# Second unit's scores ahead of the first weights, weight shifts ahead of the maximum, fewer MLP products in the step where the MLP begins

## The chip, the core and the metric

The kernel runs on one core of a Trainium2 chip. Its engines run side by side, each through its own list of instructions in order: TensorE (PE, matrix products; its weight loads are listed as PEld), VectorE (DVE), ScalarE (ACT), GpSimd (POOL) and SyncE (SP, which here only starts transfers). They wait for each other by semaphores. The metric is the device time of one execution in microseconds; the kernel before takes 1659.19 us (median of 3 runs, 1656.96 to 1659.2).

## The reference

Attention that keeps the 32 largest scores of each row, and an MLP behind it, all in float32. The input has 8 batches, 8 heads, 576 rows and a head size of 64; the MLP is 512 wide with a hidden layer of 2048.

```python
scores = scale * np.matmul(q, k.transpose(0, 1, 3, 2))
kth = np.partition(scores, -top_k, axis=-1)[..., -top_k:-top_k + 1]
scores = np.where(scores >= kth, scores, -1000000000.0)
scores = scores - np.max(scores, axis=-1, keepdims=True)
attn = np.exp(scores)
attn = attn / (np.sum(attn, axis=-1, keepdims=True) + 1e-09)
out = np.matmul(attn, v)
# [...] out goes from (B, H, S, D) to x of (B, S, H*D)
mu = np.mean(x, axis=-1, keepdims=True)
var = np.mean((x - mu) ** 2, axis=-1, keepdims=True)
xn = (x - mu) / np.sqrt(var + 1e-06) * g_ln
return x + np.maximum(xn @ w_ch1, 0.0) @ w_ch2
```

The two weight matrices arrive as float64 and are turned into float32 in the kernel from their halves of 32 bits.

## The kernel before

The work is cut into 160 units of attention: one group of up to 128 query rows for a pair of heads. One step of the main loop handles several units at different stages: it makes scores for a coming unit (PE, then ACT copies them out of PSUM), halves the next one (pairs of scores are split into the larger, `hi`, and the smaller, `lo`), selects the 32 largest of the present one (DVE), and masks, exponentiates, transposes and multiplies earlier ones. `fill()` puts products of the MLP between these parts as far as a budget allows.

**Weights.** 32 pieces of 128x512. Each is fetched, split on ACT into size, low part and sign, clamped on POOL, shifted on DVE, and joined on POOL by an addition and a product. Piece 0 to 3 come before the loop; then one or two pieces are in each step. The pieces of a step are split in that step, and shifted and joined in the next.

```python
def split(self):
    # [...] tiles size, low, sign
    nc.scalar.activation(size_f, high, AF.Abs)                                   # L183
    nc.scalar.activation(self.low[:], self.raw[:, :, 0], AF.Copy, bias=2.0, scale=2.0**-51)
    nc.scalar.activation(self.sign[:], high, AF.Sign)                            # L187
    # [...] the first 16 pieces: sign times the gain
    nc.gpsimd.tensor_scalar(size_f, size_f, HIGH_MAX, HIGH_MIN, ALU.min, ALU.max)  # L190, "clamp"

def shift(self):
    nc.vector.tensor_scalar(self.size[:], self.size[:], 3, None, ALU.logical_shift_left)  # L193

def join(self):
    nc.gpsimd.tensor_tensor(size, size, self.low[:].bitcast(U32), ALU.add)       # L199
    nc.gpsimd.tensor_tensor(self.dst, size, self.sign[:], ALU.mult)              # L201

def weights(n, phase):
    now, before = batches.get(n, []), batches.get(n - 1, [])
    if phase == 0:
        for x in batches.get(n + 1, []):
            x.fetch()
        for x in now[0::2]:
            x.split()
    elif phase == 1:
        for x in before:
            x.shift()
        for x in before:
            x.join()
        for x in now[1::2]:
            x.split()
```

**Halving.** DVE makes the maximum; POOL makes the minimum from it in two integer operations.

```python
def halve(u):
    # [...]
    nc.vector.tensor_tensor(hi, a, b, ALU.max)                                   # L375
    nc.gpsimd.tensor_tensor(lo.bitcast(I32), a.bitcast(I32), hi.bitcast(I32), ALU.subtract)  # L376
    nc.gpsimd.tensor_tensor(lo.bitcast(I32), lo.bitcast(I32), b.bitcast(I32), ALU.add)       # L379
```

**Selection.** `select(u, 0)` takes the largest of `lo` (MAX8 at L391, MATCH_REPLACE8 at L386); `select(u, 1)`, `(u, 2)`, `(u, 3)` take eight after eight from `hi` (L399, L386).

**Which scores a step makes, how much of the MLP it may fill in, and the loop:**

```python
def due(n):
    ahead = [n + 1] if n < CONVERTING else [n + 2]
    if n == CONVERTING:
        ahead = [n + 1, n + 2]
    return [units[i] for i in ahead if i < N]

def fill(least=0):
    owed[0] = min(owed[0] + share[0], 6.0)
    while todo and (not todo[0][3] or todo[0][3]()):
        if owed[0] < todo[0][1] / 2 and least <= 0:
            break
        least -= 1
        pop()

# [...] loads of the first heads
scores(units[0])
halve(units[0])
load_gain()
weights(-1, 0)
weights(-1, 1)
for n in range(END):
    now[0] = n
    if n in gives:
        give(n)               # the products of a finished block of rows enter the list
    share[0] = slot(n)
    # [...]
    for x in due(n):
        scores(x)
    if u:
        select(u, 0)
    # [...] early units: mask (L426) and exponential (L436) on ACT
    weights(n, 0)
    fill()
    # [...]
    if u:
        select(u, 1)
    if nxt:
        halve(nxt)
    for den in recips.pop(n, []):
        nc.vector.reciprocal(den, den)
    if n in turns:
        turn_heads(turns[n])  # two transposes on DVE, L306
        # [...]
    weights(n, 1)
    fill()
    # [...] mask, values, select(u, 2), transposes, select(u, 3), with fill() between
```

`gives_first` is the step in which the first block of rows enters the MLP (step 10). `CONVERTING` marks the end of the conversion.

Of the kernel before, what the change touches and what calls it, by code (L numbers as in the profile page):

```python
# [10 lines left out]
ALU = mybir.AluOpType  # L11
# [18 lines left out]
def kernel(  # L30
# [41 lines left out]
    nc = tc.nc  # L72
# [138 lines left out]
    def load_gain():  # L211
        ps = turned()
        nc.tensor.transpose(ps[:, 0:NC], grow[:], ident[0:NC, 0:NC])
        nc.scalar.copy(gcol[:], ps[:, 0:NC])


    batches = {}
# [5 lines left out]

    def weights(n, phase):

        now, before = batches.get(n, []), batches.get(n - 1, [])
        if phase == 0:
            for x in batches.get(n + 1, []):
                x.fetch()
            for x in now[0::2]:  # L230
                x.split()
        elif phase == 1:
            for x in before:
                x.shift()
            for x in before:
                x.join()
            for x in now[1::2]:
                x.split()
# [5 lines left out]
    share = [0.0]  # L244
    owed = [0.0]
# [83 lines left out]
    def scores(u):  # L329

        u.sc = scpool.tile([P, 2, S], FP32, tag="sc", name="sc")
        made = [score_half(u, s) for s in range(2)]
        for t in range(len(u.tiles)):
            for s in range(2):
                nc.scalar.copy(  # L335
                    u.sc[:, t, s * HALF : (s + 1) * HALF], made[s][t][:, 0:HALF]
                )
# [25 lines left out]
    def halve(u):  # L363

        nt = len(u.tiles)  # L370
        u.lo = lopool.tile([P, 2, HALF], FP32, tag="lo", name="lo")
        u.hi = hipool.tile([P, 2, HALF + TOP_K // 2], FP32, tag="hi", name="hi")
        a, b = u.sc[:, 0:nt, 0:HALF], u.sc[:, 0:nt, HALF:S]
        lo, hi = u.lo[:, 0:nt], u.hi[:, 0:nt, 0:HALF]
        nc.vector.tensor_tensor(hi, a, b, ALU.max)  # L375
        nc.gpsimd.tensor_tensor(  # L376
            lo.bitcast(I32), a.bitcast(I32), hi.bitcast(I32), ALU.subtract
        )
        nc.gpsimd.tensor_tensor(lo.bitcast(I32), lo.bitcast(I32), b.bitcast(I32), ALU.add)  # L379

    def select(u, i):

        nt = range(len(u.tiles))

        def replace(m, t, x):
            nc.vector.match_replace(x[:, t], m[:, t, :], x[:, t], LOWEST)  # L386

        if i == 0:
            for o in range(HALF, HALF + TOP_K // 2, 8):
                for t in nt:  # L390
                    nc.vector.max(u.hi[:, t, o : o + 8], u.lo[:, t])  # L391
                if o == HALF:
                    for t in nt:
                        replace(u.hi[:, :, o : o + 8], t, u.lo)
            return
        for r in ((0,), (1,), (2, 3))[i - 1]:
            m = small.tile([P, 2, 8], FP32, tag=f"m{r}", name=f"m{r}")
            for t in nt:
                nc.vector.max(m[:, t, :], u.hi[:, t])  # L399
            if r < TOP_K // 8 - 1:  # L400
                for t in nt:
                    replace(m, t, u.hi)
            if r == 0:
                u.top = m
            u.thr = m
# [331 lines left out]
    units = []  # L737
# [19 lines left out]
    CONVERTING = max(n for n in batches if batches[n]) + 2  # L757
# [16 lines left out]
    for j in jobs:  # L774
        if j.hp == NHP - 1:
            b = j.b
# [23 lines left out]
    def at(i):  # L800
        return units[i] if 0 <= i < N else None
# [6 lines left out]

    def due(n):

        ahead = [n + 1] if n < CONVERTING else [n + 2]
        if n == CONVERTING:
            ahead = [n + 1, n + 2]
        return [units[i] for i in ahead if i < N]
# [5 lines left out]
    for j in fresh[1:]:  # L820
        before = jobs[jobs.index(j) - 1]
# [32 lines left out]
    def slot(n):  # L854


        if n <= CONVERTING:
            return max(0.0, dve_cost(n) - pe_cost(n)) / SLOTS
        left = sum(t[1] for t in todo)
        if n > last_give:  # L860
            even = left / max(1, END - 1 - n)
        else:
            even = 99.0
            for m in sorted(gives):
                if m > n:
                    even = min(even, (left - RESERVE) / (m - n))
                    left += sum(b.cost() for b in gives[m])
        return max(0.0, even) / SLOTS
# [8 lines left out]
    gives_first = min(gives)  # L877
# [7 lines left out]
    load(fresh[1], nc.sync, nc.scalar)  # L885
    scores(units[0])
    halve(units[0])
    load_gain()
    weights(-1, 0)
    weights(-1, 1)  # L890
    for n in range(END):
        now[0] = n
        if n in gives:
            give(n)
        share[0] = slot(n)
        u, nxt, mk = at(n), at(n + 1), at(n - 1)
        ex, g = after(n)
        g = g if g and not g.quick else None
        late = at(n - 4)
        late = late if late and late.rest and late.job.b % 2 else None  # L900
        parts = turn(ex) if ex else []
        early = ex is not None and n - 1 < EARLY
        last = ex and ex is ex.group.units[-1]
        quick = ex.group if last and ex.group.quick else None

        moved = ex is not None and ex.moved
        sent, stores[:] = stores[:], []

        if ex and not early:
            weigh(ex, 0)  # L910
# [4 lines that stand above are left out]
        for store in sent:  # L915
            store()
        if n == gives_first:
            for blk, i in rows_of.pop(n):
                blk.stats(i)
        if mk and mk.i >= CONVERTING:  # L920
            prepare(mk)
        if early:
            for t in range(2):
                mask(ex, t)
                weigh(ex, t)
        if not quick:
            weights(n, 0)
        fill()
        if ex and len(ex.tiles) > 1 and not early:
            weigh(ex, 1)  # L930
        fill()
        if g:
            values(g)
        if parts and not moved:
            parts[0]()
        if ex and ex.rest:
            keep_den(ex)
        if u:
            select(u, 1)
        if nxt:  # L940
            halve(nxt)
        for den in recips.pop(n, []):
            nc.vector.reciprocal(den, den)
        if n in turns:
            turn_heads(turns[n])
            later = fresh.index(turns[n]) + 1
            if later < len(fresh):
                load(fresh[later], nc.sync, nc.sync)
        if not quick:
            weights(n, 1)  # L950
        fill()
        if mk and not early:
            mask(mk, 0)
        if g:
            place(g)
        if late:
            place_rest(late.job.b, late.job.hp)
        fill(1 if g or late else 0)
        fill()
        if len(parts) > 2:  # L960
            parts[1]()
        if u:
            select(u, 2)
        for blk, i in rows_of.pop(n, []):
            blk.stats(i)
        for blk in gives.get(n - 2, []):
            blk.inverse()
        if last and ex.group.sums is not None:
            recips.setdefault(n + 1, []).append(ex.group.sums)
        last_rest = at(n - 3)  # L970
        if last_rest and last_rest.rest and last_rest.job.b % 2:
            hp = last_rest.job.hp
            den = dr[last_rest.job.b // 2][:, 2 * hp : 2 * hp + 2]
            recips.setdefault(n + 1, []).append(den)
        fill()
        if parts:
            parts[-1]()
        if mk and len(mk.tiles) > 1 and not early:
            mask(mk, 1)
        fill()  # L980
        for x in (u if n < EARLY else None, mk if n > EARLY else None):
            if x and x is units[x.job.last]:
                load_values(x.job)
        if quick:

            values(quick)
            for den in recips.pop(n + 1):
                nc.vector.reciprocal(den, den)
            place(quick)
# [3 lines that stand above are left out]
            select(u, 3)  # L993
            if u.i < CONVERTING:
                prepare(u)
        if moved:
            move(ex)
        for x in (g, quick):
            if x and x.job.hp == NHP - 1:
                for qt in x.qts:  # L1000
                    if qt < J:
                        arrived(n, (x.job.b, qt), xs[x.job.b, qt])
        if late and late.job.hp == NHP - 1:
            r = late.job.b // 2
            arrived(n, ("r", r), rs[r])
        fill()
# [37 lines left out]
```

## Time and profile before

| engine | busy us of a span of 1655.8 | share |
|---|---|---|
| PE | 1559.2 | 94% |
| DVE | 1472.6 | 89% |
| ACT | 1036.8 | 63% |
| POOL | 673.9 | 41% |

| group | count | busy us |
|---|---|---|
| MLP, hidden products (PE, L664) | 2048 | 551.1 |
| MLP, second products (PE, L680) | 1152 | 548.7 |
| scores (PE, L354) | 1344 | 220.0 |
| largest of `hi` (DVE, L399) | 1152 | 499.4 |
| `hi` itself (DVE, L375) | 160 | 119.3 |
| `lo` on POOL (L376 and L379) | 160 each | 208.1 and 207.0 |

How to read it: PE is near full over the whole span, but an average hides stages. The span in 40 slices (tenths of busy time in each) shows the start apart from the rest:

```profile
PE   2668989989899999999999999999999999999998
DVE  5997999999999999999999999999999999997000
ACT  6986877667656666666656665666656665665310
POOL 5776763343443433344243433344343433342010
```

The first five slices, some 207 us, are those in which weights are converted: there ACT and POOL are as busy as PE, and which of the four sets the pace changes from stretch to stretch. Busy time of an engine includes the time in which one of its instructions has begun and waits inside. At the end DVE is done and PE works off the last rows of the MLP.

### The profile page before, as it was taken

What the parts mean: (1) busy time and instruction counts of PE and PEld (TensorE: products, weight loads), DVE (VectorE), ACT (ScalarE), POOL (GpSimd) and SP (SyncE); (2) the same over time, 40 slices, a digit from 0 to 9 for tenths busy, and PEclk for the clock granted to TensorE, in tenths of its full rate; (3) what the DMA queues carried; (4) which work ended last, traced back from release to release, by engine and by line L of the source; (5) the groups of instructions that cost most, each with busy time, mean ns of one, the idle gap of its engine ahead of it and who ended that gap; (6) DMA issues with size and microseconds to landing.
All of it is one profiled execution on the core that took longest, in us unless ns stands there. A gap on an engine that the chain in (4) does not pass through costs nothing.

```text
span 1655.8 us, 24475 instructions
## 1 busy us (share of the span) xinstructions
PE 1559.2 (94%) x6825; PEld 918.0 (55%) x6825; DVE 1472.6 (89%) x4619; ACT 1036.8 (63%) x2607; POOL 673.9 (41%) x879
## 2 busy tenths in 40 slices
PE   2668989989899999999999999999999999999998
PEld 1336457556355475745547575755547565755564
DVE  5997999999999999999999999999999999997000
ACT  6986877667656666666656665666656665665310
POOL 5776763343443433344243433344343433342010
PEclk9879999999999999999999999999999999999999
DMA  7422332001433334333443335233443334232000
GB/s 177 111 76 88 85 67 55 22 14 23 101 107 89 96 83 126 104 92 83 116 118 98 86 90 128 91 92 87 113 118 98 86 87 117 90 92 72 32 13 13
DMA packets 301199, 142.28 MB, mean 86 GB/s; under 512 B 246276, under 2 KB 283144, under 8 KB 301064
## 3 DMA queue, kind: packets, MB, share of 16 engines
q1 hardware_dynamic: 296328, 140.13, 31.5%
q10 hardware_dynamic: 4736, 0.59, 0.3%
q8 instruction: 55, 0.90, 0.2%
q14 instruction: 80, 0.66, 0.1%
HBM read 93.46 MB, written 47.19 MB: 85 GB/s over the span
## 4 chain that ended last, share of the span: by engine, by line
PE 71%; DVE 18%; issue 4%; ACT 4%; POOL 3%; DMA 1%; ACTq 0%; POOLq 0%; DVEq 0%
PE hps L664 25%; PE ops L680 24%; PE scps L354 8%; PE av L544 7%; DVE m L399 5%; DVE hi L386 4%; DVE hi L391 3%; PE tp L490 2%; PE av L551 2%; DVE lo L386 2%; DVE hi L375 1%; DVE size L193 1%; PE tp L648 1%; ACT sc L335 1%; PE xo L583 1%
## 5 line engine op out<-in xcount | busy, mean ns | idle before, releaser
L664 PE MATMUL hps<-xT,w 128*128 128x256 f32 (+1 forms) x2048 | 551.1, 412 | 6.1 <-ACT xT L653 6.1
L680 PE MATMUL ops<-w,h 128*128 128x512 f32 x1152 | 548.7, 603 | 0.0
L399 DVE MAX8 m<-hi 128x8 f32<-128x304 f32 x1152 | 499.4, 479 | 3.3
L664 PEld LDWEIGHTS hps<-xT,w 128*128 128x128 f32 x2048 | 373.0, 192 | 122.7 <-issue 32.1
L376 POOL TENSOR_TENSOR lo<-sc,hi 128x576 int32<-128x576 int32 (+1 forms) x160 | 208.1, 1301 | 481.9 <-DVE hi L375 225.7
L386 DVE MATCH_REPLACE8 hi<-m,hi 128x304 f32<-128x304 f32 x864 | 398.4, 477 | 0.0
L680 PEld LDWEIGHTS ops<-w,h 128*128 128x128 f32 x1152 | 200.9, 192 | 186.4 <-issue 181.4
L354 PE MATMUL scps<-kT,qT 64*128 64x288 f32 (+3 forms) x1344 | 220.0, 428 | 36.9 <-DVE qT L306 27.2
L391 DVE MAX8 hi<-lo 128x8 f32<-128x288 f32 x576 | 238.8, 458 | 12.7 <-POOL lo L379 11.6
L335 ACT COPY sc<-scps 128x288 f32<-128x288 f32 x576 | 199.5, 408 | 68.4 <-PE scps L354 54.4
L426 ACT ACTIVATE e<-sc,m 128x576 f32<-128x576 f32 x288 | 224.2, 779 | 7.6 <-DVE m L399 4.3
L436 ACT ACTIVATE e<-e,bias 128x576 f32<-128x576 f32 x288 | 224.9, 781 | 0.6
L379 POOL TENSOR_TENSOR lo<-lo,sc 128x576 int32<-128x576 int32 (+1 forms) x160 | 207.0, 1294 | 12.5
L354 PEld LDWEIGHTS scps<-kT,qT 64*128 64x128 f32 (+1 forms) x1344 | 121.7, 178 | 154.0 <-issue 60.5
L675 ACT ACTIVATE h<-hps 128x512 f32<-128x512 f32 (+1 forms) x160 | 89.1, 557 | 95.2 <-PE hps L664 94.0
L544 PE MATMUL av<-pt,vb 128*64 128x256 f32 (+2 forms) x1088 | 147.2, 413 | 0.2 <-ACT pt L513 0.2
L375 DVE TENSOR_TENSOR hi<-sc 128x576 f32<-128x576 f32 (+1 forms) x160 | 119.3, 746 | 21.3 <-ACT sc L335 21.3
L386 DVE MATCH_REPLACE8 lo<-hi,lo 128x288 f32<-128x288 f32 x288 | 127.4, 457 | 0.0
L693 POOL TENSOR_TENSOR o<-o,x 128x512 f32<-128x512 f32 x32 | 42.1, 1317 | 200.1 <-ACT o L689 200.1
L556 ACT COPY oT<-av 128x256 f32<-128x256 f32 (+2 forms) x68 | 26.2, 385 | 148.6 <-PE av L551 148.6
L544 PEld LDWEIGHTS av<-pt,vb 128*64 128x64 f32 x1088 | 73.7, 142 | 77.7 <-ACT sc L335 15.9
L490 PE MATMUL tp<-ident,e 128*128 128x128 f32 x576 | 92.0, 284 | 24.7 <-ACT e L436 24.2
(70 smaller groups left out, 1277.2 us busy)
## 6 DMA issues: line engine op xcount, KB each, us to landing
turned<-sc SPq DMA_DIRECT2D x72, 512.0 KB, 2.6
pt<-turned SPq DMA_DIRECT2D x288, 128.0 KB, 2.9
vb<-in_v_dram SPq DMA_DIRECT2D x136, 128.0 KB, 2.6
raw<-in_moe_w_ch_dram SPq DMA_DIRECT2D x32, 512.0 KB, 3.9
kin<-in_k_dram SPq DMA_DIRECT2D x128, 72.0 KB, 2.5
qin<-in_q_dram SPq DMA_DIRECT2D x120, 72.0 KB, 2.5
out_dram<-o SPq DMA_DIRECT2D x32, 256.0 KB, 2.2
ends<-in_v_dram SPq DMA_DIRECT2D x136, 16.0 KB, 2.2
```

The source lines that it names most:

```text
L335: nc.scalar.copy(u.sc[:, t, s * HALF : (s + 1) * HALF], made[s][t][:, 0:HALF])
L354: nc.tensor.matmul(ps[i * R : i * R + ql, o : o + width], qT[r, q0 : q0 + ql], kT[r, k0 : k0 + width], start=True, stop=True,)
L376: nc.gpsimd.tensor_tensor(lo.bitcast(I32), a.bitcast(I32), hi.bitcast(I32), ALU.subtract)
L379: nc.gpsimd.tensor_tensor(lo.bitcast(I32), lo.bitcast(I32), b.bitcast(I32), ALU.add)
L386: nc.vector.match_replace(x[:, t], m[:, t, :], x[:, t], LOWEST)
L391: nc.vector.max(u.hi[:, t, o : o + 8], u.lo[:, t])
L399: nc.vector.max(m[:, t, :], u.hi[:, t])
L426: nc.scalar.activation(u.e[:, t], u.sc[:, t], AF.Prelu, bias=u.thr[:, t, 7:8], scale=-1.0, alpha=SLOPE)
L436: nc.scalar.activation(u.e[:, t], u.e[:, t], AF.Exp, bias=u.bias[:, t : t + 1], scale=-scale / SLOPE, accum_out=g.den[:, col : col + 1],)
L544: nc.tensor.matmul(av[h * D : (h + 1) * D, 0 : g.nq], vb[:, h * J + c, :], g.blocks[:, h, 0 : g.nq // 32, c, :], start=(c == 0), stop=False,)
L664: nc.tensor.matmul(ps["h"][:, o : o + N], w1[:, c, f * P : (f + 1) * P], xT[0][:, c, 0:N], start=(c == 0), stop=(c == NC - 1),)
L680: nc.tensor.matmul(ps[i][:], hT[f][:, i * P : (i + 1) * P], w2[:, f, :], start=(f == 0), stop=(f == NF - 1),)
```

## The change

Three edits, all in the stretch where weights are converted.

1. The scores of unit 1 are made before the loop, ahead of the first weight splits, and step 0 makes none. `lo` of unit 0 is made by one minimum on DVE instead of two operations on POOL. It is for an earlier start of DVE's selection.
2. The shifts of a step's weights stand in front of `halve(nxt)` instead of behind it and behind the transposes of new heads. It is for keeping them away from POOL's `lo`, which begins when `hi` is done.
3. In the step in which the MLP begins, the budget is set back to zero and its share halved, so that fewer products stand in front of the next scores.

```diff
@@ weights
         elif phase == 1:
-            for x in before:
-                x.shift()
             for x in before:
                 x.join()
@@ halve
         nc.vector.tensor_tensor(hi, a, b, ALU.max)
+        if u.i == 0:
+            nc.vector.tensor_tensor(lo, a, b, ALU.min)
+            return
         nc.gpsimd.tensor_tensor(
@@ due
-        ahead = [n + 1] if n < CONVERTING else [n + 2]
+        ahead = [] if n == 0 else [n + 1] if n < CONVERTING else [n + 2]
@@ before the loop
     scores(units[0])
     halve(units[0])
+    scores(units[1])
     load_gain()
@@ the loop
         share[0] = slot(n)
+        if n == gives_first:
+            owed[0] = 0.0
+            share[0] /= 2
@@ the loop, further down
         if u:
             select(u, 1)
+        for x in batches.get(n - 1, []):
+            x.shift()
         if nxt:
             halve(nxt)
```

## The prediction

> **What bounds the kernel now.** I read four views, in this order: the busy time of the engines by stage, the waits of VectorE (DVE), the group of the moved shifts, and then the chain of waits and the timelines of the two places that the change touches. By stage (columns: stretch, length, busy time and count of TensorE (PE), its weight loads, DVE, ScalarE (ACT), GpSimd (POOL), then granted clock, DMA share, GB/s):
>
> ```profile
> 0.00:213.00 213.00, 144.71 (x602) 87.62 (x603) 181.90 (x558) 164.30 (x364) 148.66 (x138) 0.89 0.40 104
> 213.00:360.00 147.00, 136.17 (x721) 85.38 (x720) 142.33 (x453) 102.06 (x269) 64.28 (x90) 0.95 0.22 44
> 360.00:520.00 160.00, 152.62 (x692) 89.31 (x692) 156.81 (x494) 106.89 (x281) 60.74 (x94) 0.98 0.28 72
> 520.00:1480.00 960.00, 955.57 (x4213) 558.73 (x4213) 945.94 (x2973) 609.57 (x1569) 374.04 (x522) 1.00 0.36 100
> ```
>
> From 520 us to 1480 us PE is busy 955.57 of 960: that stretch keeps its length whatever happens before it, unless its work changes, and the change leaves it. So the change is worth the time by which that stretch begins earlier. All of the change lies in the first 213 us (the weights are converted in steps 0 to 17); there DVE idles 31 us. Its waits there:
>
> ```profile
> DVE hi L375 <- ACT sc L335: 21.3, 9, 7.0
> DVE kT L306 <- DMA kin<-in_k_dram: 6.5, 1, 6.5
> DVE hi L391 <- POOL lo L379: 3.0, 1, 3.0
> ```
>
> The reader is to see one long wait of 7.0 us and two at the start (the timeline has 4.2 us before the second unit's `hi` at 23.75, and the 3.0 us of L391 at 15.54). The group of the shifts, by duration:
>
> ```profile
> L193 DVE TENSOR_SCALAR size<-size x32: 392/837/1636, 25.8 to 212.8; 128x512 uint32<-128x512 uint32 x32
> ```
>
> One operation of one shape takes from 392 to 1636 ns: most of them wait inside. The chain of waits (start, us, what) shows the long wait, and one round of the steps after it:
>
> ```profile
> 125.37 13.28 PE hps L664 x52
> 138.65 1.22 PE scps L354 x8
> ...
> 140.89 0.76 DVE hi L375
> 141.65 2.31 DVE size L193 x2
> ...
> 180.12 1.56 POOL lo L376
> 181.68 0.07 issue
> 181.75 1.48 POOL lo L379
> 183.23 1.24 POOL size L199
> 184.47 0.07 issue
> 184.53 1.28 POOL w L201
> ```
>
> PE makes 26 MLP products in front of the next scores; and from 164 us on the chain runs through POOL and ACT, not through DVE.
>
> [...] a shift of 512 elements takes 392 to 430 ns when POOL is quiet, `hi` with 576 elements and two inputs 0.76 us, and the two shifts behind `hi` 2.31 us in the chain[...]. [...]
>
> **Part 1, the start.** Scores of unit 1 move in front of the first weight splits, and `lo` of unit 0 becomes one DVE minimum instead of two POOL operations. Removed: POOL's 1.41 + 1.40 us, and DVE's wait of 3.0 us. Added: one `tensor_tensor` on DVE, taken as 0.76 us like `hi`. DVE's selection of unit 0 starts at 12.5 + 0.76 = 13.3 us, not 15.54. ACT copies unit 1's scores at about 11.8 to 13.1 instead of 22.44, so the splits begin at about 13.15, not 12.75; four pieces last 9.7 us as before, to 22.85. The fourth clamp on POOL (L190) ends near 21.7, the four shifts near 22.2, `hi` of unit 1 runs at 22.2 instead of 23.75, and with two transposes (1.4 us) DVE's second select part begins at 24.3, not 30.92.
>
> I don't book these 6.6 us. The next `hi` now stands behind the shifts of pieces 4 and 5, and the clamp of piece 5 lies in POOL's queue behind four joins. POOL's joins are paced by the fifth clamp, which waits for ACT: 22.85 + 0.65 + 0.6 = 24.1; `lo` 1.41 + 0.07 + 1.40 to 27.0; four joins at 2.58 us each (33.42 to 35.99 in the timeline) to 37.3; clamp to 37.95. With POOL's next clamp of 0.6 us in front of the shift, `hi` of unit 2 runs at about 38.9 (39.13 before), and DVE goes on at 39.7 instead of 40.46. **Kept: 0.8 us.** The rest turns into a wait for POOL.
>
> **Part 2, the shifts.** All 32 take 28.2 us against 32 x 0.40 = 12.8; [...] 3.6 behind unit 1 (part of part 1), 1.7 in steps 2 to 8, about 1.6 in step 9, 8.0 in the five steps after it, 1.0 in the last two. Moved in front of `hi`, they meet no `lo`, but the POOL clamp of the next piece, and `hi` meets it too. In steps 2 to 8, where DVE has no idle time, I keep 0.6 of 1.7 (the 1.9 us pair at 81.3 us gives most). In the five steps from 141 us DVE waits for ACT's copies anyway, so DVE's 1.6 us per step are not on the chain. There a round runs: copies, ACT size 0.58, clamp 0.61, `lo` 1.56 and 1.48, join 1.24 + 1.28, then ACT's sign (which waits for that join) and about 4 us of ACT work back to the copies. `lo` alone takes 1.41 and 1.40 us: 0.24 us per round are on the chain, over six rounds **1.4 us**; of the 1.0 in the last two steps I keep **0.5**.
>
> **Part 3, fewer products.** The changed kernel's order has 6 hidden products (12 instructions) in front of the scores instead of 26. Before: products from 125.37 for 13.28 us, scores 1.22, copies done at 140.87. After, with everything 1.4 us earlier by parts 1 and 2: products from 124.0 for 12 x 0.256 = 3.1 us, scores done near 128.4. Then another thing binds: ACT's order has a split, two masks and one exponential in front of the copies, and the split's sign waits for a join on POOL that ended at 129.54 before; it begins when `lo` does, which is about the same (123.7, not 123.86), and has the faster `lo`: 129.2. Sign 0.6, masks 1.36, exponential 0.9, copies 1.2: done at 133.3 instead of 140.87, **7.5 us earlier, 6.1 more than the 1.4 already booked**. The 20 products, 20 x 2 x 0.215 = 8.6 us at full clock (four in 0.86 us in the chain at 279 us), are owed. By the order they are still 8.6 us late at the last steps of conversion; 5.2 us are caught up in three steps where the old order has next to no product left to give; 3.4 us remain over the next twelve steps. PE's waits from 213 to 360 us are 10.7 us, 5.6 of them for rows of the next MLP block, so most of it fits; the chain does run through PE from 271 to 333 us, and the order has 1.3 us more of products there. I charge **1.8 us**.
>
> **Sum:** 0.8 + 0.6 + 6.1 + 1.4 + 0.5 - 1.8 = 7.6 us earlier at 520 us, kept to the end: 1659.2 - 7.6 = 1651.6 us.
>
> **Rivals.** (a) DVE sets the pace of the whole start and all its losses come back: 6.6 at the start, 1.7 and 1.6 in steps 2 to 9, 7.0 of wait, 9 from the last steps: some 26 us, 1633 us. For it speaks that DVE is busy without a gap from 24 to 124 us; against it, POOL's queue at 38 us and the chain through POOL and ACT from 164 us. (b) PE sets the pace from 213 us on and the owed 8.6 us are paid in full: gain of 0 to 1 us, 1658 us. For it: 97% of 260 to 320 us and 99% of 360 to 440 us are PE's (58.39 of 60, 79.48 of 80 by stage); against it, the free steps and the wait of 4.35 us for rows at 342 us, where both orders are level. (c) A shift in front of `hi` waits for a clamp in other steps too[...]: some 0.5 us in each of ten steps, 1656 us.
>
> **Range and chances.** The steps at the start are sure to tenths, part 3 to about 2 us, the repayment by PE to about 3 us, rival (a) in part (a third of it) to 6 us on the fast side. The runs before spread over 2.2 us. So 1644 to 1657. 2% are 33 us, more than even rival (a): faster 0.01, within 2% 0.98, slower 0.01.
>
> **What would show it.** Right: shifts of 0.4 to 0.7 us; POOL's `lo` at 1.4 us all along; `hi` of unit 2 near 39 us with a DVE wait of 4 to 6 us in front of the shifts; copies in the step of the first block done near 133 us; rounds of 11.4 to 12.7 us after that; the last conversions 8 to 10 us earlier. Wrong: unit 2's `hi` near 33 us (then the start gives 6 us more), rounds near 10.3 us (then DVE was the bound there), or PE without gaps from 213 to 440 us and the lead gone by 520 us.

## The result and the profile after

| kernel | median us | ratio to the kernel before, 95% interval |
|---|---|---|
| before | 1659.20 | |
| changed | 1650.93 | 0.9951 [0.9933, 0.9968] |

The change makes the kernel 8.3 us faster; 7.6 were predicted. The profiled execution has a span of 1650.0 us against 1655.8. By stage, cut at the same places of the work (columns as in the prediction):

```profile
0.00:203.00 203.00, 134.58 (x576) 84.01 (x576) 172.65 (x560) 163.31 (x362) 143.80 (x136) 0.89 0.42 110
203.00:350.00 147.00, 139.91 (x745) 86.51 (x744) 140.62 (x453) 102.85 (x269) 64.80 (x90) 0.99 0.22 44
350.00:510.00 160.00, 152.85 (x696) 90.11 (x694) 154.85 (x489) 106.25 (x280) 59.79 (x94) 0.97 0.29 71
510.00:1470.00 960.00, 954.16 (x4205) 558.97 (x4204) 945.03 (x2968) 608.35 (x1568) 371.75 (x519) 1.00 0.36 100
```

By busy time TensorE has done 10.1 us less at 203 us than it had at 213 us before, and has made 3.7 us of it good by 350 us. But TensorE's busy time is no clean measure of work: in the kernel before, the 13 instructions of hidden products from 125.37 to 130.00 us took 4.63 us at a granted clock of 0.60, and the 41 from there to 138.60 took 8.60 us at 1.00. In the second stretch the clock was 0.99 against 0.95 before. By count of matrix products it is 26 behind at 203 us (576 against 602) and 2 behind at 350 us (1321 against 1323): there the owed work is made good. The waits of VectorE in the first 203 us:

```profile
DVE hi L375 <- ACT sc L335: 11.8, 7, 3.8
DVE size L193 <- POOL size L190: 11.7, 10, 4.3
DVE kT L306 <- DMA kin<-in_k_dram: 6.5, 1, 6.5
```

The wait of 7.0 us and the one for `lo` are gone. In their place stands a new row: ten times, for 11.7 us, a shift waits for POOL's clamp. The shifts themselves:

```profile
L193 DVE TENSOR_SCALAR size<-size x32: 411/427/1415, 17.1 to 201.5; 128x512 uint32<-128x512 uint32 x32
```

The median falls from 837 to 427 ns; 21 of the 32 shifts lasted over 0.5 us before, 11 do now. The chain of waits, in one round of the later steps of conversion:

```profile
157.31 1.40 POOL lo L380
158.77 1.42 POOL lo L383
160.19 1.26 POOL size L199
161.51 1.28 POOL w L201
```

The round still runs through POOL; `lo` takes 1.40 and 1.42 us instead of 1.56 and 1.48.

To follow where the time is won I use the start of `hi` of each unit, in the timeline of each kernel, as a clock: its lead is how much earlier than in the kernel before it begins. Up to unit 10 the leads of kernels whose programs are alike up to there differ by up to 2 us (0.10 to 2.06 at unit 10); from unit 11 on they repeat better (8.53 and 8.50 there for the changed kernel and for the one of experiment 7, which is alike up to there), but a difference that stood in front of unit 11 is partly carried on.

| unit of `hi` | before, us | lead, changed | without part 1 | without part 2 | without part 3 |
|---|---|---|---|---|---|
| 2 | 39.13 | 0.05 | -0.37 | 6.45 | -0.25 |
| 3 | 48.69 | 0.38 | -0.03 | 0.79 | 0.09 |
| 9 | 110.37 | 1.30 | 1.34 | -0.14 | 1.03 |
| 11 | 140.89 | 8.53 | 8.35 | 6.64 | 0.48 |
| 17 | 212.03 | 9.84 | 9.75 | 6.28 | 1.88 |
| 21 | 241.66 | 10.08 | 11.17 | 6.29 | 3.30 |
| 22 | 251.14 | 7.82 | 8.85 | 5.36 | 3.31 |
| 40 | 405.45 | 10.54 | 11.58 | 8.08 | 3.45 |
| 60 | 589.74 | 9.29 | 11.10 | 7.70 | 3.43 |
| 159 | 1509.42 | 5.82 | 7.70 | 4.35 | 3.44 |

One execution of each was profiled. Its total differs from the kernel's median by up to 2 us (without part 3 it is 2.0 us slower than the median, for the kernel before 0.9 us faster), so leads and medians can disagree by some 3 us.

### The profile page after: what moved, and what is told of

It is laid out like the page before. It is cut to its first block, busy times and chain, and to the rows that moved or that the text cites. A ratio compares the mean times of both kernels' runs of the same rounds, so it can differ in the third digit from the quotient of the medians.

```text
span 1650.0 us, 24473 instructions
## 1 busy us (share of the span) xinstructions
PE 1555.1 (94%) x6825; PEld 918.2 (56%) x6825; DVE 1461.5 (89%) x4620; ACT 1036.4 (63%) x2607; POOL 669.2 (41%) x877
## 4 chain that ended last, share of the span: by engine, by line
PE 55%; DVE 32%; issue 4%; POOL 4%; ACT 3%; DMA 1%; ACTq 0%; POOLq 0%; SPq 0%; DVEq 0%
PE hps L668 21%; PE ops L684 18%; DVE m L403 10%; DVE hi L390 8%; PE scps L354 6%; DVE hi L395 5%; PE av L548 5%; DVE lo L390 3%; DVE hi L375 2%; PE tp L494 2%; PE av L555 2%; DVE sc L472 1%; POOL lo L383 1%; POOL lo L380 1%; ACT sc L335 1%
## 5 line engine op out<-in xcount | busy, mean ns | idle before, releaser
L403 DVE MAX8 m<-hi 128x8 f32<-128x304 f32 x1152 | 488.9, 461 | 3.3
L390 DVE MATCH_REPLACE8 hi<-m,hi 128x304 f32<-128x304 f32 x864 | 390.7, 459 | 0.0
L395 DVE MAX8 hi<-lo 128x8 f32<-128x288 f32 x576 | 234.0, 443 | 11.9 <-POOL lo L383 10.8
L375 DVE TENSOR_TENSOR hi<-sc 128x576 f32<-128x576 f32 (+1 forms) x160 | 114.8, 718 | 13.2 <-ACT sc L335 13.1
L472 DVE STREAM_TRANSPOSE sc<-e 128x512 f32<-128x512 f32 x144 | 94.2, 685 | 26.4 <-ACT e L440 26.1
```

## Experiments

Each block of expectations was written before its run. All times are medians; ratios are to the kernel before.

| kernel | us | ratio, 95% interval |
|---|---|---|
| without part 1 | 1650.57 | 0.9948 [0.9933, 0.9963] |
| without part 2 | 1653.81 | 0.9969 [0.9956, 0.9982] |
| without part 3 | 1652.16 | 0.9959 [0.9944, 0.9973] |
| three pieces ahead | 1646.21 | 0.9917 [0.9900, 0.9934] |
| no budget | 1646.2 | one execution, no interval |
| four signs | 1639.76 | 0.9881 [0.9865, 0.9896] |
| caught up | 1650.78 | 0.9948 [0.9932, 0.9964] |
| three pieces, caught up | 1646.95 | 0.9923 [0.9905, 0.9941] |
| four signs, without part 2 | 1643.69 | 0.9900 [0.9885, 0.9915] |
| three pieces, four signs | 1636.63 | 0.9857 [0.9840, 0.9873] |
| three pieces, four signs, no budget | 1633.51 | 0.9838 [0.9823, 0.9852] |
| `o` behind `lo` | 1643.68 | 0.9902 [0.9886, 0.9919] |

Taken back one by one, the three parts cost -0.4, 2.9 and 1.2 us by medians, 3.7 in all of the 8.3: they do not add up. The intervals reach 2 to 3 us to either side, so of the three only the 2.9 us come near to being clear of noise.

**1. Without part 1.** The changed kernel with these lines taken back:

```diff
-        if u.i == 0:
-            nc.vector.tensor_tensor(lo, a, b, ALU.min)
-            return
-        ahead = [] if n == 0 else [n + 1] if n < CONVERTING else [n + 2]
+        ahead = [n + 1] if n < CONVERTING else [n + 2]
-    scores(units[1])          # ahead of load_gain()
```

> The change without its first part (scores of unit 1 again behind the first splits, lo of unit 0 again on POOL). Theory (POOL's four joins set the start): hi of unit 2 moves only from 39.1 to about 39.9 us, 0.8 later than in the changed kernel, and the time is about 1652. Rival (DVE sets the pace at the start, so the 6.6 us of earlier selection count): hi of unit 2 at about 44 us or the time at 1656 or more.

`hi` of unit 2 comes at 39.50 us, 0.4 later than in the changed kernel, where the theory had 0.8. At unit 17 0.1 us are left, and the time is the same, 1650.57. The rival, that VectorE sets the pace at the start, falls. The first part is worth nothing in the end: behind unit 17 this kernel is even 1 us ahead, because in the changed one unit 18 waits 1.33 us for its scores and here 0.23. Why that differs was not followed up.

**2. Without part 2.** Shifts again in `weights`, behind `hi` and the transposes:

```diff
         elif phase == 1:
+            for x in before:
+                x.shift()
             for x in before:
                 x.join()
...
-        for x in batches.get(n - 1, []):
-            x.shift()
```

> The change without its second part (shifts again behind hi and the transposes). Theory: hi of unit 2 runs as early as 32 to 33 us because no shift stands before it, but DVE then waits for the same clamp and goes on at about 39 us, so nothing is won; later the shifts take up to 1.6 us again, lo 1.5 to 1.6 us, rounds from unit 11 to 17 are 0.2 us longer each, hi of unit 17 comes about 2 us later than in the changed kernel, time about 1653. Rival (the time that shifts wait inside is all on the path): 8 to 10 us later, 1660.

The start is as the theory expected; at unit 17 it had about 2 us, and 3.6 were measured. The start in the timelines of VectorE (start, us, operation, and the idle time before it with what ended it), first without part 2:

```profile
32.68 1.74 DVE L377 TENSOR_TENSOR hi<-sc 128x576 f32<-128x576 f32 x1 [1.19 <-ACT sc L337]
34.34 1.49 DVE L193 TENSOR_SCALAR size<-size 128x512 uint32<-128x512 uint32 x1
38.94 0.82 DVE L193 TENSOR_SCALAR size<-size 128x512 uint32<-128x512 uint32 x1 [3.10 <-POOL size L190]
39.68 0.46 DVE L405 MAX8 m<-hi 128x8 f32<-128x304 f32 x1
```

and the changed kernel:

```profile
32.65 1.36 DVE L193 TENSOR_SCALAR size<-size 128x512 uint32<-128x512 uint32 x1
38.34 0.82 DVE L193 TENSOR_SCALAR size<-size 128x512 uint32<-128x512 uint32 x1 [4.33 <-POOL size L190]
39.08 0.74 DVE L375 TENSOR_TENSOR hi<-sc 128x576 f32<-128x576 f32 x1
39.75 0.46 DVE L403 MAX8 m<-hi 128x8 f32<-128x304 f32 x1
```

The order of `hi` and the shifts is swapped, `hi` is 6.4 us apart, and the selection behind both begins at 39.68 and 39.75. Both wait for the same clamp, at the end of POOL's four joins. Later the kernel without part 2 loses 1.4 us up to unit 9 (against the other kernels with parts 1 and 2 and four pieces ahead it is 1.2 to 2.3), and another 1.7 from unit 11 to 17, where a round takes 11.92 us instead of 11.64; at unit 17 the second part is worth 3.6 us, not the 8 to 10 of the rival.

**3. Without part 3.**

```diff
-        if n == gives_first:
-            owed[0] = 0.0
-            share[0] /= 2
```

> The change without its third part (26 hidden products again in front of the scores in the step where the MLP begins). Theory: DVE's wait of some 7 us in front of hi of unit 11 is back, the lead over the kernel before is 1 us there and 2 to 3 us at unit 17; no products are owed; time about 1657. Rival (TensorE gets its 8.6 us back in full later, so the third part is worth nothing): 1651 to 1652 as the changed kernel.

The wait is back (VectorE's waits from 8 to 213 us; columns: in total, times, longest):

```profile
DVE hi L375 <- ACT sc L335: 19.2, 8, 7.2
```

The chain explains the 7.2 us, and shows the 26 products of the prediction once more:

```profile
124.58 13.59 PE hps L668 x52
138.17 1.22 PE scps L354 x8
```

At unit 11 the changed kernel is 8.05 us ahead of this one, at unit 17 7.96; 0.5 us of it stood already at unit 10 (leads of 0.62 and 0.10), where the two programs don't differ yet. But this one's lead over the kernel before stays flat to the end (3.31 at unit 22, 3.44 at 159), while the changed kernel's falls from 10.1 to 5.8. By the leads 2.4 us of the third part are left at the last unit, by the medians 1.2. The time, 1652.2 us, was missed; 1657 had been expected. Part 3 is worth 8 us where it acts and 1 to 2 at the end. Experiments 5, 7 and 10 look for the rest.

**4. Three pieces ahead of the loop.**

```diff
-        count = 4 if n < 0 else 1 + (n + 1) % 2 if n < NF // 2 else 2
+        count = 3 if n < 0 else 2 if n < 2 else 1 + (n + 1) % 2 if n < NF // 2 else 2
```

> The changed kernel with three weight pieces ahead of the loop instead of four, and two in step 1 instead of one: POOL has three joins in front of the clamp that DVE waits for. Theory (that clamp sets the start): the clamp ends near 33 us instead of 38.3, hi of unit 2 runs at about 33.8 instead of 39.1, and 4 to 5 us of it stay at units 4 to 17; time about 1647. Rival (ACT's splits, transfers or DVE itself set it): hi of unit 2 not before 38 us, time unchanged.

```profile
30.64 1.04 DVE L193 TENSOR_SCALAR size<-size 128x512 uint32<-128x512 uint32 x1
33.41 0.82 DVE L193 TENSOR_SCALAR size<-size 128x512 uint32<-128x512 uint32 x1 [1.74 <-POOL size L190]
34.15 0.74 DVE L375 TENSOR_TENSOR hi<-sc 128x576 f32<-128x576 f32 x1
```

The wait for the clamp falls from 4.33 to 1.74 us, `hi` of unit 2 comes at 34.15 instead of 39.08, 3.8 us of that are left at unit 17 and 5.2 at the last unit; 1646.2 us. With one join less the start is shorter: what held it was the clamp behind the joins.

**5. No budget in the step where the MLP begins.** `share[0] = 0.0` instead of `share[0] /= 2`. The six products and the transposes of the MLP's rows stand behind the scores.

> The changed kernel with no budget at all in the step where the MLP begins: its six hidden products and the transposes of the MLP's rows also go behind the scores. Theory (with six products the path already runs through POOL's join and ACT's sign, no longer through TensorE): hi of unit 11 stays at 132.4 us, at most 0.5 earlier. Rival (TensorE's products still set it): 3 us earlier, 129.4.

`hi` of unit 11 came at 130.89 us, 1.5 earlier. But its lead was already 2.06 instead of 0.62 at unit 10, in front of the edited step; across the step the lead grows by 7.94 us, against 7.91 in the changed kernel. So the step itself gains nothing, as the theory has it: with six products TensorE is off the path. What binds is ACT's sign, which waits for POOL's join. ACT's waits from 120 to 140 us, in the changed kernel and then without a budget:

```profile
ACT sign L187 <- POOL w L201: 6.6, 2, 4.5
```

```profile
ACT sign L187 <- POOL w L201: 5.4, 1, 5.4
```

The round behind it takes 14.30 us instead of 11.84, and at unit 17 the lead is 8.25, less than the 9.84 of the changed kernel. TensorE makes 33 instructions of hidden products in that round, where it makes 28 in the changed kernel, and the granted clock from 130 to 140 us was 0.61 in this execution against 1.00; which of the two made it longer isn't separated. The 4.7 us at the end (one execution) are not from this step: of its lead of 11.5 at the last unit, against 5.8, 2.9 appear at unit 22 (10.69 against 7.82, where `lo` waits in the changed kernel as experiment 10 shows) and more at late units.

**6. Four buffers for the sign tiles.** For pieces of the second weight matrix there are three; ACT's sign of a piece waits for the join of the piece three before. The fourth is a tile that attention uses only after the conversion.

```diff
-                pl, tag = ((opool, "o"), (opool, "o"), (rpool, "r"))[self.i % 3]
+                pl, tag = ((opool, "o"), (opool, "o"), (rpool, "r"), (restpool, "all"))[self.i % 4]
...
-                    oTr[hp] = restpool.tile([P, P], FP32, tag=f"oTr{hp}", name="oTr")
+                    if not oTr:
+                        every = restpool.tile([P, DM], FP32, tag="all", name="oTr")
+                        for x in range(NHP):
+                            oTr[x] = every[:, x * P : (x + 1) * P]
```

> The changed kernel with a fourth buffer for the sign tiles of the second weight matrix, so that ACT's sign no longer waits for the join of this same step. Theory (rounds of units 11 to 17 run in a ring through copies, clamp, lo, join, sign and back): ACT's 16.5 us of waits for that join fall below 4, the six rounds fall from 12.0 to about 11 us on the mean (TensorE's work per round is 10.6), hi of unit 17 comes 4 to 6 us earlier, time 1647 to 1649. Rival (POOL's own work or TensorE sets the rounds): rounds stay at 12, time as the changed kernel.

ACT's waits from 128 to 205 us, in the changed kernel:

```profile
ACT sign L187 <- POOL w L201: 16.5, 7, 4.5
```

and with four signs, its whole list:

```profile
ACT x L564 <- DVE den L960: 2.5, 1, 2.5
ACT sc L335 <- PE scps L354: 2.1, 2, 1.9
ACT low L184 <- POOL w L201: 0.7, 1, 0.7
ACT oT L560 <- PE av L555: 0.5, 1, 0.5
ACT size L183 <- POOL size L199: 0.5, 1, 0.5
```

The 16.5 us are gone and the six rounds fall from 11.64 us on the mean (my 12.0 was the mean of the longer five) to 10.31. The lead at unit 17 grows from 9.84 to 18.51, and the kernel takes 1639.8 us, 7 to 9 below what I expected. The ring through POOL's join was the bound of these rounds. The granted clock isn't the cause: from unit 11 to 17 it was 0.93 in the changed kernel and 1.00 with four signs, but 0.98 in the kernel without part 1, whose rounds still take 11.62 us.

**7. Caught up.** The 20 owed products are made in the last four steps of conversion, and TensorE's order is that of the kernel before again from step 26 on.

```diff
             share[0] /= 2
+        if CONVERTING - 3 <= n <= CONVERTING:
+            share[0] += 0.27
```

> The changed kernel with a larger budget in the last four steps of conversion (0.27 us more for each of eight fillings), so that the 20 owed products are made there and the order of TensorE's products is the one of the kernel before from step 26 on. Theory (the lead of the changed kernel falls from 10.1 us at unit 21 to 5.8 at the last unit because its later order of products meets other small waits): 1 to 3 us are lost at units 15 to 20, then the lead stays flat, as it does without the third part; 7 to 9 us at the last unit, time 1647 to 1649. Rival (the owed work itself is paid on a full TensorE): the lead at the last unit is 5 to 6 us and the time 1651.

The lead falls from 9.34 at unit 15 to 7.05 at unit 21, is 7.36 at unit 34, and then stays flat: 7.02 at unit 159. So the owed work costs some 2 us when it is repaid at once, and the later fading of the changed kernel's lead belongs to its order of products. The time is not better (1650.78): repaying at once costs what the order costs.

**8. Three pieces and caught up.**

> Three pieces ahead of the loop together with the larger budget in the last four steps of conversion. Theory: the two add up (the lead of three pieces over the changed kernel is 5.2 us at the last unit, that of the budget 1 to 3): 1642 to 1645. Rival: no better than three pieces alone, 1646.

8.71 us of lead at the last unit against 11.03 without the catching up; 1646.95 us. The two don't add up: unit 17 has 13.67 without and 12.33 with, unit 18 14.64 and 10.64. The theory's sum was wrong, and the time is the rival's. Why the repayment costs more here isn't shown: from unit 16 to 19 TensorE has no gap in either kernel (26.28 of 26.31 us busy, in experiment 7 25.32 of 25.35), and in the two rounds ahead of that the granted clock was 0.93 against 0.98.

**9. Four signs without part 2.** Both edits as above.

> Four sign buffers, first and third part of the change, but the shifts again behind hi. Theory (with three buffers the ring through POOL's join hid the 1.6 us per step that shifts wait inside; with four DVE sets the rounds, so it counts): rounds of units 11 to 17 rise from 10.1 us with shifts in front to about 11.5, hi of unit 17 comes 8 to 10 us later than in that kernel (the second part is worth 3.6 there with three buffers), time 1647 to 1650. Rival (the shifts' inner wait never counts): 3.6 us later at unit 17, time 1643.

The theory missed, and so did the rival's 3.6 us at unit 17; the rival's time, 1643, is what was measured. At unit 17 the lead is 18.22, against 18.51 with the shifts in front; at the last unit it is 2.9 us less, by medians 3.9. The rounds take 10.20 us without part 2 and 10.31 with it. Busy time from 131.7 to 193.5 us, without part 2 and then with it:

```profile
131.70:193.50 61.80, 61.50 (x318) 41.73 (x318) 61.66 (x198) 60.40 (x139) 57.39 (x51) 1.00 0.33 97
```

```profile
131.70:193.50 61.80, 60.86 (x314) 40.13 (x312) 59.13 (x194) 58.13 (x134) 55.17 (x49) 1.00 0.35 97
```

Without part 2 VectorE has no gap, and the chain of waits in this stretch runs through VectorE alone:

```profile
by line: DVE m L405 29.3%; DVE hi L392 26.8%; DVE hi L397 13.1%; DVE size L193 13.0%; DVE hi L377 8.3%; DVE lo L392 7.8%; DVE bias L421 2.4%; DVE den L959 0.3%; issue 0.2%
```

With part 2 the chain goes through ACT, POOL and VectorE, with the two operations of POOL's join ahead (12.4% and 12.1%). So the theory was right that VectorE would set these rounds once the ring is open; it was wrong in the length, for which it had 11.5 us. VectorE needs 10.20, about what POOL and ACT take in the other kernel. TensorE is close behind in both (61.50 and 60.86 of 61.80 us) and isn't excluded as a limit of its own. What part 2 is worth here shows only when conversion ends.

**10. `o` behind `lo`.** POOL adds the residual to a finished row block (`o`), and that addition waits for ACT and for TensorE's last product of the block. It is held back until the next `hi` and `lo` are issued.

```diff
-                    nc.gpsimd.tensor_tensor(o[:], o[:], self.x[i], ALU.add)
-                    for dst, rows in self.dsts[i]:
-                        stores.append(...)
+                    add_now()             # one that is still held back
+                    adds.append(add)      # add(): the same two statements
...
         if nxt:
             halve(nxt)
+        add_now()
```

> The changed kernel with POOL's addition of the residual (o) held back until the next hi and lo are issued, so that lo never stands behind an o that waits for TensorE's last product of a block. Theory (part of the changed kernel's lead fades because its later order of products puts such an o in front of lo: DVE waits 3.0 us at unit 22 and 2.8 us at unit 157): both waits go, the lead at unit 22 stays near 10 us instead of 7.8, and the last unit comes 2 to 5 us earlier; time 1646 to 1649. Rival (TensorE is full and takes these waits back at once): no more than 1 us, 1650 to 1651.

POOL around unit 22, in the changed kernel and then with `o` held back:

```profile
235.22 1.27 POOL L697 TENSOR_TENSOR o<-o,x 128x512 f32<-128x512 f32 x1 [6.73 <-ACT o L693]
236.44 1.41 POOL L380 TENSOR_TENSOR lo<-sc,hi 128x576 int32<-128x576 int32 x1
237.93 1.41 POOL L383 TENSOR_TENSOR lo<-lo,sc 128x576 int32<-128x576 int32 x1
```

```profile
232.30 1.40 POOL L386 TENSOR_TENSOR lo<-sc,hi 128x576 int32<-128x576 int32 x1 [3.88 <-DVE hi L381]
233.78 1.41 POOL L389 TENSOR_TENSOR lo<-lo,sc 128x576 int32<-128x576 int32 x1
235.15 1.28 POOL L706 TENSOR_TENSOR o<-o,x 128x512 f32<-128x512 f32 x1
```

In the first, `hi` had ended at 232.33 us, and `lo` stood behind an `o` that waited until 235.22. VectorE's waits for `lo` from 203 to 1500 us fall from the first line to the second:

```profile
DVE hi L395 <- POOL lo L383: 10.8, 10, 3.0
```

```profile
DVE hi L401 <- POOL lo L389: 1.6, 4, 0.4
```

The lead is 11.04 at unit 22 instead of 7.82, and 15.88 at unit 159 instead of 5.82: 10 us, at least twice what I expected; 1643.7 us. The rival, that TensorE takes these waits back, falls. From unit 19 to 159 VectorE waits 9.2 us less for `lo`, 3.9 us more for ACT's exponential (7.2 to 11.1), and is busy 4.7 us less (1259.98 to 1255.27), most of it in `hi`. Together that is the 10 us.

**11. The best of them together.** Three pieces and four signs, and the same without a budget in the first MLP step.

> Three pieces ahead of the loop and four sign buffers. Theory (one shortens the start, the other the rounds from unit 11 on): the two add up, hi of unit 17 22 us before that of the kernel before, time about 1634.6. Rival (the rounds are then bound by fetches or TensorE and take the 5 us back): 1639.

> Three pieces ahead, four sign buffers and no budget in the step where the MLP begins. Theory (the six products were not on the path, and a later order of products changes the end by 2 us either way): 1632 to 1637. Rival (the budget itself brought the 4.7 us of the one look without it): 1630.

1636.6 and 1633.5 us: the sum of the first theory (22 us at unit 17, 1634.6) is missed by 2 us, the second held. At unit 17 three pieces add only 1.8 us to four signs, not 3.8; at unit 10, in front of the rounds, the leads were 3.6 with both and 1.8 with four signs alone, and the rounds are equally long (10.30 and 10.31 us). At unit 9 the leads had been 5.8 and 1.9; why three pieces lose 2 us from there to unit 10 was not followed up. The last kernel is the fastest measured, 26.3 us below the kernel before in the same series (1659.79). Holding `o` back was not tried together with it.

## Why the prediction held, point by point

That the total came out at 1650.9 for 1651.6 is partly luck: its terms are further off, and their errors offset each other.

- **"Kept: 0.8 us" (part 1).** At unit 2 the working held: clamp ended at 38.31 (I had 37.95), `hi` at 39.08 (38.9), selection at 39.75 (39.7), and VectorE waits 4.33 us in front of the shift. That the other 6 us turn into a wait for POOL is shown by experiments 1, 2 and 4. But the 0.8 themselves don't last: 0.1 at unit 17, nothing in the time. The term is mis-sized by 0.8.
- **"I keep 0.6" and "1.4 us" and "0.5" (part 2).** Measured against the kernel without it: 1.4 up to unit 9, 0.5 to unit 11, 1.7 over the six rounds; 3.6 in all at unit 17 where I had 2.5. The 0.6 was too small. It was taken from the losses that part 2 lists by steps (3.6, 1.7, 1.6, 8.0 and 1.0 us), an estimate of mine of what the shifts in the trace last beyond 0.40 us each. The 1.4 for the rounds held: they are 1.3 us shorter than in the kernel before. That the 1.6 us inside each step don't count in the later rounds was right: those rounds are 11.84, 11.86, 12.69, 12.35, 11.56 and 9.54 us, and experiment 6 shows what held them.
- **"7.5 us earlier, 6.1 more" (part 3).** The copies end at 132.32 us (133.3 predicted); the lead over the kernel without it grows by 7.5 us from unit 10 to unit 11, so the 6.1 was some 1.4 us too small. That another thing binds from there, not the six products, is shown by experiment 5: ACT's sign waits there for POOL's join.
- **"I charge 1.8 us" for the owed products, and "keeps its length whatever happens before it".** The repayment alone costs about 2 us (experiment 7), and its course was right: by count 20 second products (0.43 us each) are still owed at unit 17 and none at unit 32. The step that failed is the second one: from unit 60 to 159 the changed kernel takes 923.14 us, the kernel before 919.68, although that stretch has the same work. VectorE is busy for 905.75 and 905.47 us of it; what grows is its waiting, from 7.6 to 10.9 us. The waits of VectorE, before (589.74 to 1509.42 us) and changed (580.45 to 1503.60 us):

```profile
DVE hi L391 <- POOL lo L379: 4.2, 5, 1.5
DVE sc L468 <- ACT e L436: 3.4, 6, 0.9
```

```profile
DVE sc L472 <- ACT e L440: 6.0, 6, 2.6
DVE hi L395 <- POOL lo L383: 4.9, 4, 2.8
```

Most of it (2.6 us) is waiting for ACT's exponential and only 0.7 us for `lo`. TensorE waits more too, 6.9 us instead of 4.1. So a TensorE that is 99% busy did not fix the length of that stretch: it follows the order of products, by small waits on both engines; which of the two sets the pace there isn't separated. The kernels whose order becomes that of the kernel before again (without part 3, experiments 7 and 8) keep their lead from unit 40 to 159 within 0.4 us. The others lose 1.6 to 5.1 us there, but for the one with `o` held back, which gains 2.1. Part 3 lost 5.6 us of its 8 to this and to the repayment, where I charged 1.8. How much `o` has in it by itself isn't separated: holding it back also removes waits that the kernel before had, such as 2.6 us at 355 us.

- **Rivals.** (a) fell: without part 1 the time is the same. (b) was half right for another reason: most of part 3 is gone at the end, but not because TensorE is full. (c) was right in kind: seven shifts in front of `hi` wait 0.51 us each for a clamp, but that falls into time in which VectorE would wait for ACT.

So the terms that were too small (1.4 us in part 3, 1 in part 2) and those too large (0.8 in part 1, some 4 of fading) offset each other.

## What to carry to other kernels

An instruction that waited held what stood behind it in its engine's queue: in the changed kernel `lo` was held from 232.3 to 236.4 us by an `o` in front of it. Look for instructions whose input comes from a distant engine (the clamp behind four joins, the residual addition in front of `lo`) and put what others wait for in front of them. When a round runs in a ring through two engines, ask which buffer closes it: one more tile brought more than the whole change (11.2 us against 8.3). And follow a gain by the same mark in both traces to the end, because a saving of 8 us at the start was 1 to 2 at the end, with the work in between unchanged.

## What the runs showed of the hardware

A shift on VectorE that runs into an operation of POOL can be recorded as busy for longer, not as idle: the same shift lasts 0.39 to 1.64 us. In the kernel before 21 of the 32 last 0.51 to 1.64 us, and each of them ends 0.28 to 0.29 us after the end of an operation of POOL that had begun before it; the other 11 last 0.39 to 0.43 us. In the changed kernel the same holds for 11 of 0.58 to 1.42 us, and the shifts that no operation of POOL overlaps last 0.41 to 0.43 us. The two shifts behind `hi` that take 2.31 us in the prediction's chain last 0.84 us, to 142.41 (POOL's clamp ends at 142.13), and 1.63 us, to 143.95 (`lo` ends at 143.67); the record has the second begin at 142.33, with `lo` still running. In the rounds with four signs and without part 2, where VectorE reads 61.66 of 61.80 us busy, 8.0 us of the chain are its 12 shifts.

It goes both ways: POOL's clamp of 0.61 us lasts 1.59 us (at 47.93 us in the changed kernel, where it ends 0.47 us after `hi`) or 1.85 us (at 39.17 us in the kernel before, where it ends 0.47 us after the second shift). That the excess is time spent waiting is my reading of where these records end; what would hold an instruction isn't in them.
